# A delta-rule attention and gMLP kernel: one written-out list of steps, 16x16 blocks joined on TensorE, packed grams, loads in halves

## The chip, the cores and the metric

The kernel runs on one core of one Trainium2 chip. Its engines here are TensorE (PE, with PEld for its weight loads), VectorE (DVE), ScalarE (ACT), GpSimd (POOL) and SyncE (SP, which only issues DMAs). The metric is device microseconds (us) of one execution, lower is better; the median of the runs is compared.

## What is computed

Attention with the delta rule runs over 768 tokens for 4 x 8 heads with 48 dimensions, then a gated MLP with a matmul over the tokens:

```python
k_n = k / (norm(k) + 1e-06)
for t in range(S):                                    # S = 768, state is 48x48 per head
    y[:, :, t] = einsum('bhd,bhde->bhe', q[:, :, t], state)
    v_old = einsum('bhde,bhd->bhe', state, k_n[:, :, t])
    state = state + bt * einsum('bhd,bhe->bhde', k_n[:, :, t], v[:, :, t] - v_old)
x = y.transpose(0, 2, 1, 3).reshape(B, S, H * D)      # 4 x 768 x 384
h = gelu_tanh(x @ w_in)                               # 1024 columns
u, v = h[..., :512], h[..., 512:]
v_n = (v - mean(v)) / sqrt(var(v) + 1e-06) * g_ln
v_s = einsum('ts,bsd->btd', w_sg, v_n) + b_sg[None, :, None]
return x + (u * v_s) @ w_out
```

## The kernel before

**Tiling.** The 768 tokens are cut into 12 chunks of 64 tokens, six for each of two batch halves (phases). A chunk holds 32 heads as 16 pairs `j` on 128 partitions, and its pairs come in two groups e = 0 and 1 (two batches that the state passes through one after the other). Two chunks are a segment. Inside a chunk the recurrence is solved with the inverse of a 64x64 unit triangular matrix per head, built from the gram matrix of the keys.

**The inverse.** `kgram` and `gram` make the grams on PE; ACT copies them to `gm` (L225, L272, L295); `gstore` (L240) sends their 32x32 diagonal blocks to DRAM (`gd`, 64 KB each, four per chunk); `zload` (L306) brings them back as `zl`, one 32x32 block per partition. `lanes(g)` then inverts all blocks of a group of segments at once on DVE: norms by Newton steps (L176 to L184), `scale` (L352), an elimination over 30 pivots with `row` (L357), `column` (L362), `outer` (L368) and `add` (L375), `last` (L396). Groups 0 and 1 are one segment each (chunks 0 and 1, chunks 2 and 3), groups 2 and 3 two segments each. `zstore` (L421) writes the blocks to `zd`, and `zfetch` reads them per chunk: two DMAs for `zk` (L430), four for the tile `z` (L435). `turned` transposes `zk` on DVE (L444). `corner_a` and `corner_b` compute the off-diagonal 32x32 quarter on PE, 32 matmuls each, with an ACT copy `j` (L461) between and four ACT copies of `z` behind (L478).

**The chain of a chunk.** For e = 0 and 1: `old` (PE, then DVE adds into `v`, L510), `own` (PE, ACT copies `u`, L532), `state` and `read` (PE, ACT copies `s`, L545, and `x`, L560). The state `s` of one step feeds the next `old`. All these matmuls stand on one line of a helper, L81, as do the grams and corners.

**The MLP.** `Ffn(c)` of a finished chunk: `turn` (transposes L664, `xh` on ACT, `xl` on DVE L668), `values` (18 matmuls, L678, gelu on ACT, `bn_stats` on DVE), `gate` (four times nine matmuls, L642 to L644, gelu L699). The weight `w_in` comes in six pieces that DVE decodes, about nine operations each (L584 to L602, ACT cast L594). After the last chunk come the norm, the matmul over tokens (`spatial`) and the output (`project`); this tail is the same code in both kernels.

**What sets the order.** The program is written in the order in which each engine runs it. `TURNS` says which chunk's chain runs with which chunk's `Ffn`; a fixed body places every step of a turn. The DVE work of `lanes` and the decoding stand in a list `bg`, and `tick` lets them out by a budget of microseconds per step (`SHARE`, `COST`). Nearly all DMAs are issued by SP, in program order: a DMA whose data isn't there holds all behind it. The fetch of `z` for a chunk is made at the head of the turn if its segment is stored by then, and again at its end.

Of the kernel before, what the change touches and what calls it, by code (L numbers as in the profile page):

```python
# [50 lines left out]
TURNED = {0: 0, 1: 1, 3: 2, 4: 3, **{c + 2: c for c in range(4, NCH)}}  # L51
# [3 lines left out]
def delta_rule_gmlp_kernel(  # L55
# [63 lines left out]
    GM = [(main if i < 4 else low).tile([P, NP, 2, T], F32, name=f"gm{i}") for i in range(N_M)]  # L119
# [19 lines left out]
    loads = [nc.sync]

    def kload(c):
        if c < NCH:
            load(loads[0], KD[c % N_2], kqT[c])

    def qload(c):
        if c < NCH:
            load(loads[0], KQ[c % N_2], kqT[c])

    def tload(c):
        if c < NCH:  # L150
            load(loads[0], KT[c % N_2], ktok[c])

    def vload(c):
        if c < NCH:
            load(loads[0], V[c % N_2], vtok[c])

    bg, credit = [], [0.0]

    def tick(us):

        credit[0] += us
        while bg and credit[0] >= bg[0][1]:
            f, cost = bg.pop(0)
            credit[0] -= cost
            f()
        if not bg:
            credit[0] = 0.0
# [44 lines left out]

    def kgram(c):
        def phase(e):
# [16 lines left out]
    def gstore(c, queues):  # L231
# [5 lines left out]
        for half in range(2):  # L237
            for sd in range(2):
# [39 lines left out]
    def gram(c):  # L278
# [4 lines left out]
        def phase(qd):  # L283
# [10 lines left out]
            def done():  # L294
                nc.scalar.copy(out=GM[c % N_M][:, js], in_=st["ps"])  # L295
# [5 lines left out]
    def zload(s):  # L301
        if s >= NSEG:
            return
        if s % 2 == 0:
            zsrc[0] = prep.tile([P, 2, 32, 32], F32, name="zl")
        nc.sync.dma_start(  # L306
            out=zsrc[0][:, s % 2], in_=gdt.pop(s).rearrange("a b c j s t -> (a b c j) s t"))

    def lanes(g):
# [5 lines left out]
        st = {}  # L315

        n = prep.tile([P, m, 32], F32, name=f"n{m}", bufs=2)
        nb = prep.tile([P, m, 32], F32, name=f"nb{m}")
        d0 = prep.tile([P, m, 32], F32, name=f"d0{m}")
        tv = nc.vector  # L320

        def triu():
            (nc.scalar.copy if g < 1 else tv.tensor_copy)(out=d0, in_=dg)
            for a in range(m):
# [3 lines left out]
                )  # L328

# [35 lines left out]

        def outer(i, r0, r1, at):
            w = 31 - i
            tv.tensor_tensor(  # L368
                out=st["tmp"][:, at:at + m * (r1 - r0) * w].rearrange("p (m r t) -> p m r t", m=m, t=w),
                in0=z[:, :, r0:r1, i:i + 1].broadcast_to([P, m, r1 - r0, w]),  # L370
                in1=z[:, :, i:i + 1, i + 1:32].broadcast_to([P, m, r1 - r0, w]), op=ALU.mult)

        def add(i, r0, r1, at):
            w = 31 - i
            tv.tensor_tensor(  # L375
                out=z[:, :, r0:r1, i + 1:32], in0=z[:, :, r0:r1, i + 1:32],
                in1=st["tmp"][:, at:at + m * (r1 - r0) * w].rearrange("p (m r t) -> p m r t", m=m, t=w),
                op=ALU.add)

        us = lambda n: (0.13 if m == 1 else 0.17) + n / 960  # L380
        ops = [(f, us(32 * m)) for f in first] + [(scale, m * us(1024))]
        for i in range(1, 31):
            w = 31 - i
            if i <= N_ROWS[m]:
                ops += [(lambda a=a, r=r, i=i: row(a, r, i), us(w)) for r in range(i) for a in range(m)]
            elif w <= N_COLS[m]:
                ops += [(lambda a=a, t=t, i=i: column(a, t, i), us(i)) for t in range(i + 1, 32) for a in range(m)]
            else:
                parts = [(0, i // 2, 0), (i // 2, i, 256)] if m == 1 else [(0, i, 0)]
                ops += [(lambda i=i, p=p, f=f: f(i, *p), us(m * (p[1] - p[0]) * w)) for f in (outer, add) for p in parts]  # L390
            if g == 0 and i == 28:
                ops.append((lambda: tv.tensor_copy(out=kick[:, 0:8], in_=z[:, 0, 0, 20:28]), us(8)))
# [752 lines left out]
```

## Time and profile before

| what | value |
|---|---|
| median of 3 runs | 538.41 us (537.6 to 540.06) |
| the profiled execution: its own time is its span | 538.2 us |
| PE busy | 441.4 us (82%) |
| DVE busy | 346.6 us (64%) |
| ACT busy | 171.8 us (32%) |
| POOL busy | 74.9 us (14%) |
| chain that ended last | PE 61%, DVE 17%, DMA 7%, issue 7%, ACT 4%, SP's queue 4% |

The page of the profile gives each engine's busy time and the chain of work that ended last, followed back from the last instruction. The shares are averages; the stages differ, and the stretches below are cut at events of the program: the first operation of the first inversion (18.7 us), its store (47.2), the second `v` add of chunk 3 (155.9), the first of chunk 4 (200.4) and the start of the last part's steady run (378.0).

### The profile page before, as it was taken

The page shows a single profiled execution, that of the slowest core. Times are in us where ns is not written, and L with a number is a line of the kernel's source. Part 1 is how long each engine was busy: PE and PEld are TensorE (multiplying, and loading weights), DVE is VectorE, ACT ScalarE, POOL GpSimd, SP SyncE. Part 2 cuts the span into 40 slices and gives each one's busy share as a digit, 9 for nine tenths or more (in the row PEclk, how much of TensorE's full clock was granted, in tenths as well). Part 3 has the DMA queues.
Part 4 walks back from the last instruction along what each step waited for, and adds up shares of the span by engine and source line. Part 5 has one row for each costly group of instructions (what it writes and reads, how often), then busy time and mean ns, then how long its engine had stood idle before and what let it go on. Part 6 is the DMA issues. An engine that isn't in the chain of part 4 may idle for free.

```text
span 538.2 us, 17698 instructions
## 1 busy us (share of the span) xinstructions
PE 441.4 (82%) x7691; PEld 395.2 (73%) x7691; DVE 346.6 (64%) x858; ACT 171.8 (32%) x383; POOL 74.9 (14%) x87
## 2 busy tenths in 40 slices
PE   4316785570889949898989896999998999999997
PEld 2316475470778748687777775878898999999997
DVE  3999999648997229689913359643599636623332
ACT  3222333230423522333533533444534213211110
POOL 2100002102201004010010110000024223222130
PEclk9555756555599969899999998899999999999999
DMA  7987858965538796645955868265857753344204
GB/s 181 278 199 195 179 156 211 248 174 126 156 95 237 218 206 165 195 117 165 314 146 155 277 154 250 65 202 163 246 161 187 214 166 104 103 147 147 74 16 132
DMA packets 111965, 93.18 MB, mean 173 GB/s; under 512 B 74768, under 2 KB 88016, under 8 KB 111888
## 3 DMA queue, kind: packets, MB, share of 16 engines
q1 hardware_dynamic: 101504, 68.23, 45.3%
q0 software_dynamic: 6032, 22.28, 15.0%
q10 hardware_dynamic: 4352, 1.54, 1.2%
q8 instruction: 60, 0.98, 0.8%
q14 instruction: 17, 0.14, 0.1%
HBM read 63.69 MB, written 28.34 MB: 171 GB/s over the span
## 4 chain that ended last, share of the span: by engine, by line
PE 61%; DVE 17%; DMA 7%; issue 7%; ACT 4%; SPq 4%; ACTq 1%; DVEq 0%
PE ps L81 19%; PE ps L642 12%; PE ps L644 11%; PE ps L643 11%; PE ps L678 8%; DVE ztmp L368 3%; DVE zl L375 3%; DMA kd<-kqT 2%; DMA vraw<-vD 2%; PE ps L664 1%; DMA gd<-gm 1%; DMA zl<-gd 1%; SPq L752 1%; ACT gm L295 1%; DVE zl L357 1%
## 5 line engine op out<-in xcount | busy, mean ns | idle before, releaser
L81 PEld LDWEIGHTS ps<-s,kq 48*64 48x64 f32 x1408 | 55.8, 159 | 21.3 <-issue 14.8
L81 PE MATMUL ps<-s,kq 48*64 48x48 f32 x1408 | 63.1, 245 | 9.7 <-issue 8.3
L785 POOL TENSOR_TENSOR ga<-ga,uT 128x384 f32<-128x384 f32 x32 | 36.3, 1140 | 165.8 <-DVE ga L782 120.9
L81 PE MATMUL ps<-kd 48*64 48x128 f32 (+1 forms) x768 | 40.2, 337 | 19.4 <-DMA kd<-kqT 17.4
L81 PE MATMUL ps<-v,z 64*64 64x48 f32 x768 | 33.7, 244 | 23.2 <-DVE v L510 13.8
L81 PEld LDWEIGHTS ps<-kd 48*64 48x64 f32 x768 | 33.8, 177 | 22.9 <-DMA kd<-kqT 15.3
L81 PEld LDWEIGHTS ps<-v,z 64*64 64x64 f32 x768 | 30.4, 159 | 24.5 <-DVE v L510 14.4
L368 DVE TENSOR_TENSOR ztmp<-zl 128x120 f32<-128x120 f32 (+25 forms) x132 | 45.9, 372 | 2.2
L375 DVE TENSOR_TENSOR zl<-zl,ztmp 128x120 f32<-128x120 f32 (+25 forms) x132 | 45.7, 370 | 1.6
L642 PE MATMUL ps<-xh,winh 128*128 128x256 f32 x144 | 45.7, 317 | 0.9 <-DVE xl L668 0.9
L643 PE MATMUL ps<-xl,winh 128*128 128x256 f32 x144 | 42.1, 293 | 0.4 <-DVE xl L668 0.3
L644 PE MATMUL ps<-xh,winl 128*128 128x256 f32 x144 | 41.8, 290 | 0.0
L647 ACT CAST gh<-ga 128x384 fp32r<-128x384 f32 x32 | 16.3, 511 | 77.3 <-POOL ga L785 63.3
L81 PE MATMUL ps<-u,gm 64*64 64x48 f32 x768 | 34.1, 245 | 2.6 <-ACT u L532 1.9
L648 DVE TENSOR_TENSOR gl<-ga,gh 128x384 fp32r<-128x384 f32 x32 | 18.1, 565 | 26.8 <-ACT gh L647 26.7
L532 ACT COPY u<-ps 128x384 f32<-128x384 f32 x24 | 11.5, 479 | 70.6 <-PE ps L81 70.6
L644 PE MATMUL ps<-wouth,gl 128*128 128x384 f32 x96 | 32.3, 340 | 1.5 <-DVE gl L648 1.5
L81 PEld LDWEIGHTS ps<-u,gm 64*64 64x64 f32 x768 | 30.2, 159 | 4.4 <-ACT u L532 2.4
L642 PE MATMUL ps<-wsgh,vnh 128*128 128x384 f32 x96 | 32.7, 340 | 0.7 <-ACT vnh L755 0.6
L81 PE MATMUL ps<-u,kt 64*48 64x48 f32 x704 | 27.3, 234 | 6.4 <-issue 4.6
L643 PE MATMUL ps<-wsgl,winh 128*128 128x384 f32 x96 | 32.5, 339 | 0.0
L642 PE MATMUL ps<-wsgh,winh 128*128 128x384 f32 x96 | 32.5, 339 | 0.0
(127 smaller groups left out, 1097.2 us busy)
## 6 DMA issues: line engine op xcount, KB each, us to landing
kq<-kqT POOLq DMA_DIRECT2D x10, 896.0 KB, 6.8
uD<-ut SPq DMA_DIRECT2D x12, 512.0 KB, 5.2
vD<-vg SPq DMA_DIRECT2D x24, 256.0 KB, 4.0
vraw<-vD SPq DMA_DIRECT2D x48, 128.0 KB, 3.1
uT<-uD SPq DMA_DIRECT2D x8, 768.0 KB, 5.4
kd<-kqT SPq DMA_DIRECT2D x6, 896.0 KB, 8.3
xD<-x SPq DMA_DIRECT2D x12, 384.0 KB, 6.9
x<-xD SPq DMA_DIRECT2D x48, 96.0 KB, 2.8
```

The costliest lines, as they stand in the source:

```text
L81: return nc.tensor.matmul(out=out, lhsT=lhsT, rhs=rhs, start=start, stop=stop, skip_group_check=True)
L295: nc.scalar.copy(out=GM[c % N_M][:, js], in_=st["ps"])
L368: tv.tensor_tensor(out=st["tmp"][:, at:at + m * (r1 - r0) * w].rearrange("p (m r t) -> p m r t", m=m, t=w), in0=z[:, :, r0:r1, i:i + 1].br ...
L375: tv.tensor_tensor(out=z[:, :, r0:r1, i + 1:32], in0=z[:, :, r0:r1, i + 1:32], in1=st["tmp"][:, at:at + m * (r1 - r0) * w].rearrange("p (m ...
L532: ins = mark(nc.scalar.copy(out=u[:, js[e]], in_=ub[e]))
L642: nc.tensor.matmul(out=ps, lhsT=sh, rhs=mh, start=(first and i == 0), stop=False)
L643: nc.tensor.matmul(out=ps, lhsT=sh, rhs=ml, start=False, stop=False)
L644: nc.tensor.matmul(out=ps, lhsT=sl, rhs=mh, start=False, stop=(last and i == n - 1))
L647: nc.scalar.copy(out=hi, in_=src)
L648: nc.vector.tensor_tensor(out=lo, in0=src, in1=hi.bitcast(F32), op=ALU.subtract)
L678: nc.tensor.matmul(out=self.ps, lhsT=(self.xl if k == 2 else self.xh)[:, cc, bi], rhs=(winl if k == 1 else winh)[:, cc, DH:], start=(i == ...
L785: nc.gpsimd.tensor_tensor(out=gv, in0=gv, in1=uT[:, :, d], op=ALU.mult)
```

## The change

- **One list.** `TURNS`, `tick`, `SHARE` and `COST` are gone. `PROGRAM` is a list of 490 words such as `old:0:4` or `l:22` (the next 22 operations of `lanes` in `bg`) or `d:1` (the next part of the decoding), done one by one. Every load and store names its queue, S (SP), A (ACT) or P (POOL). DMAs issued by SP go from 353 to 303, by ACT from 10 to 54, by POOL from 37 to 68.
- **16x16 blocks.** For groups 0 and 1 `lanes` inverts two 16x16 blocks per 32x32 block: 28 multiplies and adds in a row. `join` makes the 32x32 inverses from them for chunks 0 to 3, on PE, with two masked copies and an add on DVE and four ACT copies per chunk; both halves of `zk` are fetched and transposed there.
- **Packed grams.** `gm` is split in keys (packed in 32-token halves) and queries. Two neighbouring heads then stand side by side, and a corner takes 16 matmuls instead of 32; `corner_a` ends in a masked copy on DVE (L504) instead of the ACT copy, `corner_b` in two ACT copies instead of four. Each quarter of a gram is copied by two ACT copies (L236, L331) instead of one.
- **Loads.** `kd` and `kq` are loaded in halves of 448 KB; each load waits for the last marked copy (of `u` or `s`) before it in the list. `z` is fetched once per chunk.
- **Moved.** No decoding stands ahead of the first inversion; the first `values` and `gate` steps stand inside the chain of chunk 2, not of chunk 3.

```diff
-TURNS = ((0, None), (1, None), (2, None), (3, 0), (None, 1), (None, 2),
-         *((c, c - 1) for c in range(4, NCH)), (None, NCH - 1))
+PROGRAM = """
+keys:1:S keys:0:A consts beta:A kq:1:0:P kq:1:1:S kgram:0 kgram:1 kd:3:1:S gstore:0:S:A gstore:1:P kd:3:0:P kq:0:0:S
+kick:12 zload:0:A kd:2:1:A l:1 kd:2:0:A qgram:1 lanes:0 gram:3 kd:5:0:P gram:2 warm:9 kq:0:1:P w:0:A kt:0:P
...
+l:6 turn:2 v:4:S kt:4:S vprep:4 l:2 kd:11:0:A own:1:3 l:1 ustore:0 gate:1:0 values:1:17 gate:1:1 kd:10:0:S
+gstore:8:S:P gstore:9:S:P kd:11:1:P kq:5:1:P state:1:3 gate:1:2 gate:1:3 v:5:P ustore:1 gate:2:0 gram:11 gate:2:1
+blocks:4:S:P l:5 xstore:2 heads:4:S:A:P gate:2:2 gate:2:3 turn:3 values:2:16 mask:7 kt:5:S corner_a:4 gram:10 turned:4
+gstore:10:S mask:6 old:0:4 zload:4:S vprep:5 mask:8 gate:3:0 values:2:1 heads:5:S:P corner_b:4 norms:3 gstore:11:S
...
+        if marked:
+            tc.add_manual_dep(
+                ins.ins, marked[0].ins.name,
...
+        nblk, w0 = (2 * m, 16) if small else (m, 32)
...
         def outer(i, r0, r1, at):
-            w = 31 - i
+            w = w0 - 1 - i
             tv.tensor_tensor(
-                out=st["tmp"][:, at:at + m * (r1 - r0) * w].rearrange("p (m r t) -> p m r t", m=m, t=w),
-                in0=z[:, :, r0:r1, i:i + 1].broadcast_to([P, m, r1 - r0, w]),
-                in1=z[:, :, i:i + 1, i + 1:32].broadcast_to([P, m, r1 - r0, w]), op=ALU.mult)
+                out=products(i, r0, r1, at),
+                in0=zb[:, :, r0:r1, i:i + 1].broadcast_to([P, nblk, r1 - r0, w]),
+                in1=zb[:, :, i:i + 1, i + 1:w0].broadcast_to([P, nblk, r1 - r0, w]), op=ALU.mult)
...
+        def one(half):
+            ps = bank().rearrange("p (i x t) -> p i x t", x=2, t=32)
+            for i in range(8):
+                for sd in range(2):
...
+                    mm(ps[TOK[sd], i], g[b, half, x].rearrange("p x t -> p (x t)"),
+                       z[b, x, 32 * half:32 * half + 32])
+            y[half] = main.tile([P, 8, 2, 32], F32, name="j1", bufs=2)
+            head_pairs(y[half], ps, same_upper)
...
         for i in range(8):
-            for odd in range(2):
-                for sd in range(2):
-                    a = slice(64 * sd + 32 * odd, 64 * sd + 32 * odd + 32)
-                    b = slice(64 * sd + 32, 64 * sd + 64)
-                    j = 2 * i + odd
-                    mm(ps[a, i], g[b, j, 0, 0:32], z[b, j, 32:64])
-        nc.scalar.copy(out=j1, in_=ps)
+            for sd in range(2):
+                b = slice(64 * sd + 32, 64 * sd + 64)
+                x = slice(2 * i, 2 * i + 2)
+                mm(ps[TOK[sd], i], g[b, 0, x].rearrange("p x t -> p (x t)"), z[b, x, 32:64])
+        head_pairs(j1, ps, same)
```

On DVE, at the first elimination, where `zl` holds the blocks, `ztmp` the products and `nb` the factors per token, the kernel before has, behind its `scale`:

```order
L352 TENSOR_TENSOR zl<-zl,nb_253 128x1024
L357 SCALAR_TENSOR_TENSOR zl<-zl 128x30
L357 SCALAR_TENSOR_TENSOR zl<-zl 128x29 x2
L357 SCALAR_TENSOR_TENSOR zl<-zl 128x28 x3
L357 SCALAR_TENSOR_TENSOR zl<-zl 128x27 x4
```

and the changed kernel, at the same place:

```order
L396 TENSOR_TENSOR zl<-zl,nb_285 128x2x16x16
L420 TENSOR_TENSOR ztmp<-zl 128x28
L427 TENSOR_TENSOR zl<-zl,ztmp 128x2x14
L420 TENSOR_TENSOR ztmp<-zl 128x52
L427 TENSOR_TENSOR zl<-zl,ztmp 128x2x2x13
```

The 36 single rows and columns and 76 halves of products and adds have become 28 operations, each on both small blocks of all partitions.

On SP's queue, around the fetch of chunk 4's blocks (`z_104` and `zk`), the kernel before has:

```order
L240 DMA gd<-gm_98 32x16x32 x4
L685 DMA vD_75<-vg 128x512
L430 DMA zk<-zd 64x8x32 x2
L435 DMA z_104<-zd 32x16x32 x4
L704 DMA uD_77<-ut 128x2x512
L685 DMA vD_75<-vg 128x512
L240 DMA gd<-gm_99 32x16x32 x4
L685 DMA vD_75<-vg 128x512
L430 DMA zk<-zd 64x8x32 x2
L435 DMA z_104<-zd 32x16x32 x4
```

and the changed kernel, where the other half of these fetches stands on POOL's and ACT's queues:

```order
L267 DMA gd<-gm_97 32x16x32 x2
L807 DMA uD_77<-ut 128x2x512
L470 DMA zd<-zl 128x1024 x2
L476 DMA z_104<-zd 32x16x32 x2
L812 DMA xD_73<-x 128x2x384
L476 DMA zk<-zd 64x8x32
L788 DMA vD_75<-vg 128x512
```

The second fetch of the same blocks, behind the store of the last gram `gm_99`, is gone, and the fetch stands right behind the store `zd`.

On ACT, between the two copies `u` of chunk 0's chain, the kernel before has:

```order
L532 COPY u<-ps 128x384
L545 COPY s_112<-ps 112x384
L560 COPY x<-ps 128x384
L295 COPY gm_102<-ps 128x512
L532 COPY u<-ps 128x384
```

and the changed kernel:

```order
L638 COPY u<-ps 128x384
L267 DMA gd<-gm_100 32x16x32 x2
L721 DMA ut<-w_in 128x2x512
L651 COPY s_112<-ps 112x384
L666 COPY x<-ps 128x384
L172 DMA kd_95<-kqT 112x2x512
L638 COPY u<-ps 128x384
```

DMA issues now stand on ACT between the copies on which the chain of the chunks hangs.

## Rows read from the trace of the kernel before

**Rows 1.** The page: busy us of each engine, share of the span, instructions.

```profile
PE 441.4 (82%) x7691; PEld 395.2 (73%) x7691; DVE 346.6 (64%) x858; ACT 171.8 (32%) x383; POOL 74.9 (14%) x87
```

**Rows 2.** Stretches: length, busy us by engine, granted clock, DMA share, GB/s.

```profile
0.00:18.70 18.70, 6.11 (x137) 3.12 (x137) 9.91 (x20) 4.91 (x8) 3.58 (x13) 0.82 0.72 193
18.70:47.20 28.50, 13.05 (x317) 12.40 (x321) 27.43 (x133) 6.91 (x16) 1.23 (x1) 0.56 0.89 242
47.20:155.90 108.70, 70.28 (x1948) 59.94 (x1941) 91.12 (x248) 34.80 (x78) 14.65 (x18) 0.58 0.72 175
155.90:200.40 44.50, 36.27 (x602) 31.34 (x601) 21.87 (x45) 17.51 (x43) 1.44 (x2) 0.92 0.74 198
200.40:378.00 177.60, 161.25 (x3830) 135.40 (x3831) 111.96 (x260) 70.89 (x177) 17.70 (x22) 0.96 0.63 182
378.00:538.20 160.20, 154.46 (x869) 153.01 (x867) 84.32 (x155) 36.73 (x63) 36.34 (x32) 1.00 0.46 141
```

**Rows 3.** Timeline of DVE: first and last operation of the first elimination (start, us).

```profile
24.66 1.48 DVE L357 SCALAR_TENSOR_TENSOR zl<-zl 128x30 f32<-128x30 f32 x8
...
45.79 0.09 DVE L400 MEMSET zl<- 128x32 f32 x1
```

**Rows 4.** Groups of DVE by line and shape: count, busy us, mean ns of one.

```profile
L396 DVE TENSOR_TENSOR zl<-zl,nb 128x1024 f32<-128x1024 f32 x6 | 7.1, 1213 | 0.0
L444 DVE STREAM_TRANSPOSE ztk<-zk 128x256 f32<-128x256 f32 x12 | 5.3, 438 | 3.5 <-DMA zk<-zd 3.5
L598 DVE TENSOR_TENSOR ut<-ut,vg 128x512 f32<-128x512 f32 x6 | 4.2, 693 | 0.2
L368 DVE TENSOR_TENSOR ztmp<-zl 128x112 f32<-128x112 f32 x4 | 1.1, 266 | 0.0
```

**Rows 5.** What DVE waited for, 47.2 to 155.9: us in total, times, longest.

```profile
DVE d L323 <- DMA zl<-gd: 8.6, 1, 8.6
DVE vg L584 <- DMA ut<-w_in: 3.8, 1, 3.8
```

**Rows 6.** Timeline of DVE: chunk 3's second `v` add, chunk 4's first.

```profile
155.87 0.55 DVE L510 TENSOR_TENSOR v<-v,ps 128x384 f32<-128x384 f32 x1
...
200.44 0.56 DVE L510 TENSOR_TENSOR v<-v,ps 128x384 f32<-128x384 f32 x1 [5.36 <-PE ps L81]
```

**Rows 7.** Timeline ahead of chunk 4: last gram store, fetch, first corner (idle before, releaser).

```profile
188.41 2.01 SPq L240 DMA_DIRECT2D gd<-gm  x4
...
191.00 1.29 SPq L430 DMA_DIRECT2D zk<-zd  x2
...
195.67 1.29 PE L81 MATMUL ps<-z,gm 32*32 32x32 f32 x64 [6.81 <-DMA z<-zd]
```

**Rows 8.** The chain of waits, 150 to 180: start, us, what.

```profile
156.89 1.08 PE ps L81 x64
...
166.36 0.12 PE ps L644
...
167.91 1.84 PE ps L678 x8
```

**Rows 9.** Timeline of PE at full clock: a whole gram, a corner.

```profile
173.43 1.98 PE L81 MATMUL ps<-kd 48*64 48x128 f32 x64
...
279.38 0.75 PE L81 MATMUL ps<-z,gm 32*32 32x32 f32 x64
```

**Rows 10.** What PE waited for, 200.4 to 378.

```profile
PE ps L81 <- issue: 11.4, 10, 2.6
```

**Rows 11.** Timeline of ACT and PE around ACT's issues of chunk 0's fetch.

```profile
50.54 1.39 ACTq L435 DMA_DIRECT2D z<-zd  x2
51.97 1.56 ACT L295 COPY gm<-ps 128x512 f32<-128x512 f32 x3 [7.86 <-issue]
...
52.61 1.75 PE L81 MATMUL ps<-kd 48*64 48x128 f32 x26 [2.03 <-ACT gm L295]
```

**Rows 12.** A stretch inside the first elimination, columns as in Rows 2.

```profile
20.00:30.00 10.00, 6.11 (x137) 5.78 (x141) 9.35 (x48) 4.76 (x12) 0.00 (x0) 0.67 1.09 292
```

More of the change, by code (lines that the diff above doesn't have):

```diff
@@ new lines @@
+old:0:1 gstore:6:S:A:P d:2 kd:8:1:A own:0:1 turned:2 join:1:2 d:2 gram:7 join:2:2 state:0:1 kq:2:0:S old:1:1 d:1
+own:1:1 mask:4 join:3:2 turn:0 mask:2 v:2:S corner_a:2 state:1:1 d:1 blocks:3:S:P turn:1 join:0:3 gstore:7:S:A:P
+corner_b:2 d:2 join:1:3 heads:3:S kd:9:0:A kd:8:0:P zload:2:P turned:3 zload:3:S bglanes:2 gram:8 v:3:S d:1 l:1
+kq:2:1:A kd:9:1:S l:2 vprep:2 xstore:1 old:0:2 gram:9 kt:2:A join:2:3 kq:3:0:S own:0:2 l:3 kq:3:1:A l:1 kd:10:1:S l:22
+l:3 vprep:3 values:0:6 join:3:3 state:0:2 old:1:2 gate:0:0 own:1:2 l:12 kt:3:P corner_a:3 state:1:2 old:0:3 l:10
@@ L135, in load, with behind @@
         flat = tile.rearrange("p j t -> p (j t)") if len(tile.shape) == 3 else tile.rearrange("p i j t -> p (i j t)")
-        q.dma_start(
+        ins = q.dma_start(
             out=flat.rearrange("p (n x) -> p n x", x=src.shape[-1]), in_=src.rearrange("n p x -> p n x"))
[L139 to L167, printed above, removed]
+        if marked:
+            tc.add_manual_dep(
+                ins.ins, marked[0].ins.name,
+                mybir.DependencyInfo(mybir.DependencyClass.Sync, mybir.DependencyReason.DATA),
+                reason="loads are spread over the turn")
+    queues = {"S": nc.sync, "A": nc.scalar, "P": nc.gpsimd}
+    bg = []
+    def behind(n):
+        for _ in range(min(n, len(bg))):
+            bg.pop(0)[0]()
     def until(ready):
@@ L373, in add @@
         def add(i, r0, r1, at):
[L374 to L378, printed above, removed]
+            z_ = zb[:, :, r0:r1, i + 1:w0]
+            tv.tensor_tensor(out=z_, in0=z_, in1=products(i, r0, r1, at), op=ALU.add)
         us = lambda n: (0.13 if m == 1 else 0.17) + n / 960
-        ops = [(f, us(32 * m)) for f in first] + [(scale, m * us(1024))]
@@ L388, in lanes @@
             else:
[L389 to L392, printed above, removed]
+                parts = [(0, i // 2, 0), (i // 2, i, 256)] if m == 1 and not small else [(0, i, 0)]
+                ops += [(lambda i=i, p=p, f=f: f(i, *p), us(nblk * (p[1] - p[0]) * w) + (0.08 if small else 0.0))
+                        for f in (outer, add) for p in parts]
@@ L818, in delta_rule_gmlp_kernel, with keys, make_constants, first_keys @@
+    ffns, chains, joins, units, held, units_w = {}, {}, {}, [], {}, []
+    def keys(c, q):
+        load(q, KD[c % N_2][:, 0], kqT[c, 0:2])
+    def make_constants():
+        make_identity(nc, ident)
+        for z in Z:
+            for r in range(2):
+                nc.gpsimd.memset(z[64 * r + 32:64 * r + 64, :, 0:32], 0.0)
+    def first_keys(c):
         k0, k1 = kgram(c)
         deal([k0], [k1])
[L820 to L822 removed]
@@ new lines, in link, with chain_of, joined, transposed @@
+    def link(name, c, new=None):
+        chain_of(c, new)[name]()
+    def chain_of(c, new):
+        if c not in chains:
+            chains[c] = chain(c, new)
+        return chains[c]
+    def joined(k, c):
+        if c not in joins:
+            joins[c] = join(c)
+        joins[c][k]()
+    def transposed(c):
+        ffns[c] = Ffn(c)
+        ffns[c].turn()
+    def gated(c, d):
+        decoded(len(win) - 9)
+        ffns[c].gate(d)
+    def valued(c, n):
+        decoded(len(win))
+        ffns[c].values(n)
@@ new lines, in key_norms, with decoded, all_lanes, lanes_in @@
+    def key_norms(s):
+        until(lambda: s in ns)
+        norms(s)
+    def decoded(n):
+        for _ in range(n):
+            win.pop(0)[0]()
+    def all_lanes(g):
+        for op, _ in lanes(g):
+            op()
+    def lanes_in(s, q):
+        if s % 2 == 0 and s:
+            lanes_done(s - 1)
+        zload(s, q)
+    def blocks_in(c, qs):
+        lanes_done(c // 2)
+        zblocks(c, spread(qs))
+    def heads_in(c, qs):
+        lanes_done(c // 2)
+        zheads(c, spread(qs))
```

569 lines of the change are left out of this document (266 added, 303 removed).

## The prediction, made before the changed kernel ran

> **What bounds the kernel now.** I read the page's busy line first, then the stretches, then inside each stretch what its late engine waits for. PE is busy for 441.4 us of 538.2 [rows 1], so the whole gain to be had by removing idle time is under 97 us, and the stretches say where those lie [rows 2]. In the last one PE works 154.5 of 160.2 us at clock 1.00: nothing to gain. From 200.4 to 378.0 it works 161.3 of 177.6 at 0.96. From 155.9 to 200.4 it works 36.3 of 44.5, and 6.8 of what is missing is one wait, ahead of chunk 4's first corner, for the blocks `z` [rows 7]. Before 155.9 PE is no bound: 89.4 of 155.9 busy, at clock 0.56 to 0.58 for most of it, while DVE is 27.4 of 28.5 and 91.1 of 108.7 busy. So DVE's queue sets when chunk 3 ends, chunk 4's blocks then set when PE can go on, and from there PE is the bound. I cut the run at DVE's `v` adds [rows 6] and write it as A (start to chunk 4's first add, 200.4) + B (to 378.0, 177.6) + C (160.2) = 538.2, the profiled execution's own time; the median of the runs, 538.41, is 0.2 above it.
>
> **A, DVE up to chunk 3's second add (155.9).** *Small blocks.* An elimination took from 24.66 to 45.79 plus 0.09, 21.1 us [rows 3]. The new one is 28 operations, 2240 elements per partition in all. From the 112 and 512 element rows [rows 4], 0.266 and 0.693 us, an operation costs about 0.149 + n/960, so 28 x 0.149 + 2.33 = 6.5. Each waits for the one ahead, where the old halves overlapped; no row prices that apart, so I bound it by 0 and 0.1 us each and take 0.04: 7.6 (6.5 to 9.3). `scale` and `last` fall from 1.21 (the row of 1024 elements, [rows 4]) to 0.69, 1.0 for the pair. That is 14.5 per group; two groups, **-29.0**. *Added.* A joined chunk costs DVE two masked products of 512 elements (0.69 each), a second transpose (0.44) and a small add (under the 0.27 of 112 elements plus what PSUM adds; 0.3): 2.1, four chunks **+8.5**. The masked corner copy moves from ACT to DVE, 0.69 x 4 = **+2.8** here (x 12 in all). One mask is taken a chunk earlier, 1024 elements, **+1.2**. *Moved.* The decoding that stood ahead of the first elimination filled a wait: DVE was 9.9 us busy in 0 to 18.7 [rows 2], and about 10 of that now follows the elimination, **+10**. Is the elimination then earlier? It waits for the grams' trip through DRAM, which remains; I leave its start at 18.7 (17 to 21). The sum is -6.5 of DVE work. Idle time in this part was 12.4 us in two waits [rows 5], one for the blocks of lanes, one for a piece of `w_in`; the same two loads remain in another order, so I keep it (6 to 20). So 155.9 - 6.5 = **149.4** (143 to 157). The large eliminations of groups 2 and 3 are not touched.
>
> *Is PE able to follow?* It gets the joins: per chunk 64 + 64 + 32 passes of 32 columns or fewer, at the corner's 0.75 per 64 [rows 9] up to 1.9 us, at half clock 3.8, four times 15. It gets some 14 `values` and 3 `gate` steps that stood behind 155.9: at 0.23 (1.84 for 8) and 1.1 (nine at 0.12) [rows 8], doubled for the clock, 6.4 + 6.6. 89.4 + 15 + 13 = 117 us of work in 149.4: it fits, but no longer loosely. ACT gets sixteen-row copies and twice the gram copies, at under 0.15 us more per pair: 35 us of 108.7 was its load [rows 2].
>
> **A, from there to chunk 4 (44.5 before).** At full clock I count what stands in the new list between `old:1:3` and `old:0:4`: 33 `values` x 0.23 = 7.6; 8 gates x 1.2 = 9.6; two whole grams x 1.98 [rows 9] = 4.0; two turns, own, state, old and the corner, by the 1.08 of 64 passes [rows 8], about 6. That is 27 to 28, against some 34 by the same count before, plus the waits. The 6.8 for `z` [rows 7] goes if the blocks are there: the second elimination pair ends as far behind chunk 3's second add as before, 16 us of DVE work, so at about 166; a store and a fetch then need some 8 (the fetch took 191.0 to 195.7 [rows 7], the store by its position about 3): 174. The corner comes about 25 us behind 149.4, at 174. So it is met, just; what is late next is the corner itself. Fetching once, ahead of the last gram store (188.4 [rows 7]), is what makes that possible. 149.4 + 28 = **177** (171 to 188), against 200.4.
>
> **B.** Seven corners: 32 passes of 64 columns instead of 64 of 32. Passes took 11.7 ns at 32 columns [rows 9], 16.9 at 48 [rows 8] and 31 at 128 [rows 9], so I take 20 at 64: 0.64 against 0.75, 0.11 twice per chunk, -1.6; the ACT copies behind them get shorter too, in all **-2**. PE's idle time is 16.3, of it 11.4 in ten waits at issue [rows 10], and 4% of clock on 161 us is 6 more. A new interleaving moves these; nothing in a row says by how much, so between 0 and two thirds (15) I take **-6**, since no wait is long (2.6 at most) and DVE with 112 of 177.6 is no bound. 177.6 - 8 = **169.6** (163 to 178).
>
> At the corners a rule speaks for more. The rows say that passes follow their columns. The Trainium skill, "TensorEngine Tiling (Array Packing)", section "Instruction Overhead", states that each matmul has about 60 cycles of overhead and that one column costs as much as 60. By it halving the calls would halve the corners, 0.75 in place of 0.22 saved per chunk, and the sum would be 3.7 lower; the trace disagrees between 32 and 48 columns.
>
> **C.** The last part is the same code with PE at 154.5 of 160.2: **160.2** (159 to 162).
>
> **Sum: 177 + 169.6 + 160.2 = 507 us.** By the ends of the three parts, which need not fall together, 493 to 528.
>
> **Rivals.**
> *PE's gaps close.* If the new list also fills the waits that I kept (chunk 4 at 171, the lower end, and B at 163): 171 + 163 + 160.2 = **494** (485 to 497). For it: PE worked 70 of 108.7 us at half clock in the middle, so there is room. Against: it needs DVE's waits gone, too.
> *PE and DVE wait in turn.* The 28 us of joins and early MLP work may not fit under DVE's queue, since chain steps need one engine, then the other, and PE had 38.4 idle in 47.2 to 155.9 [rows 2] for that reason. If half of it adds up, chunk 4 is at 177 + 14.5 = 191.5 and the time is **522** (515 to 533). For it: DVE's and PE's loads are 131 and 117 of 149.
> *The DMA engines are the bound early.* Their share was 0.72 to 0.89 up to 200 [rows 2] and 1.09 in 20 to 30 [rows 12]; the change cuts eliminations, not bytes. Then lanes start no earlier, halves or not, A stays at 200.4 and only B's 8 is gained: **530** (530 to 539); without B's gain no change. For it: the three long waits named above are all for a DMA. Against: 0.72 from 47.2 to 155.9 leaves a quarter of the engines' time. The Trainium skill, "DMA: Bandwidth & Descriptors", section "Issuing engines are not separate DMA queues", says that DMAs of ScalarE, SyncE and GpSimd run on the same 16 engines and that more issuers only save issue time; it speaks for this rival, and no row here, with nearly all issues on SP, shows it.
> *Slower: ACT as an issuer.* When ACT issued the fetch of chunk 0's blocks, its gram copies stood 7.86 us behind, and PE 2.03 behind them [rows 11]. The new list puts 22 issues on ACT between the first join and chunk 4's corner, between copies of `u` and `s`, each waiting for a landing or for the DMA eight issues earlier. If each costs the chain that 2.03, 45 us come on top: **552**. It decides from 1.55 us per issue on ((541.1 - 507) / 22). Against: most of these waits are for landings long past when ACT arrives.
>
> **How the numbers follow.** Forecast 0.45 (497 to 515), gaps closed 0.15, waiting in turn 0.20, DMA bound 0.08, ACT as issuer 0.12. A change of under 0.5%, 2.7 us (535.7 to 541.1), can't be told from none by runs that spread over 2.5. Faster: 0.45 + 0.15 + 0.20 and a quarter of 0.08: 0.82. Same: the rest of the DMA case, 0.06. Slower: 0.12. The range goes from 488, which leaves out the lower part of the closed gaps, to 536, which leaves out the ACT case and the DMA case's upper part: 0.8 lie inside.
>
> **What would show it.** Right: the first elimination starts near 18.7 and takes 8 us; chunk 3's second add near 149, chunk 4's first near 177, with no long wait of PE for `z` ahead of it; the last part 160 long. Wrong: idle time of ACT ahead of `u` or `s` behind its own issues (the slower case); a first elimination well behind 21, or waits of DVE for `zl` above 12 us (DMA); PE and DVE both under 80% busy from 50 to 150 with waits on each other (in turn); `z` of chunk 4 landing behind 180, then the second half of the gain in A is lost.

## The result, and the profile after

The changed kernel takes 513.85 us (median of 4, 512.55 to 516.31) against 538.0 beside it: ratio 0.9545, 95% interval 0.9501 to 0.9589, 24.5 us faster. The forecast was 507 (488 to 536). Medians are of all executions, ratios only of those in the chip's faster state. The profiled execution took 510.8 us, against 538.2, so 27.4 have to be found there.

The page of the changed kernel, busy time and the chain that ended last by engine:

```profile
PE 452.8 (89%) x7563; PEld 414.5 (81%) x7563; DVE 332.4 (65%) x728; ACT 171.8 (34%) x403; POOL 92.7 (18%) x120
...
PE 74%; DMA 13%; DVE 7%; ACT 3%; issue 2%; SPq 1%; POOL 0%; ACTq 0%; POOLq 0%; DVEq 0%
```

PE is busy for 11 us more than in [rows 1], and the run is shorter: PE's idle time fell from 97 to 58 us. The two `v` adds at which the prediction cut the run, in DVE's timeline of the changed kernel:

```profile
154.82 0.55 DVE L616 TENSOR_TENSOR v<-v,ps 128x384 f32<-128x384 f32 x1 [0.48 <-PE ps L115]
...
181.63 0.54 DVE L616 TENSOR_TENSOR v<-v,ps 128x384 f32<-128x384 f32 x1
```

Chunk 3's second add stands where it stood [rows 6], 1.05 us earlier; chunk 4's first is 18.8 earlier. The rest is shown by cutting both runs at these adds and at the first matmul over the tokens. First the kernel before, then the changed one (columns as in [rows 2]; a granted clock of 1.00 is 2.4 GHz, 0.50 is 1.2 GHz):

```profile
0.00:155.87 155.87, 89.42 (x2394) 75.44 (x2395) 128.43 (x398) 46.59 (x102) 19.46 (x31) 0.61 0.75 190
155.87:200.44 44.57, 36.34 (x602) 31.41 (x602) 21.90 (x45) 17.54 (x43) 1.44 (x2) 0.92 0.74 198
200.44:378.88 178.44, 162.09 (x3834) 136.08 (x3834) 112.60 (x262) 71.74 (x179) 17.70 (x22) 0.96 0.63 182
378.88:538.20 159.32, 153.58 (x865) 152.29 (x863) 83.67 (x154) 35.88 (x60) 36.34 (x32) 1.00 0.46 141
```

```profile
0.00:154.82 154.82, 112.75 (x2844) 98.67 (x2845) 112.46 (x267) 55.22 (x148) 37.69 (x61) 0.77 0.71 190
154.82:181.63 26.81, 26.81 (x443) 24.34 (x444) 20.56 (x41) 12.23 (x34) 5.33 (x8) 1.00 0.89 268
181.63:354.30 172.67, 160.31 (x3415) 139.08 (x3414) 118.90 (x275) 70.56 (x164) 14.00 (x19) 0.97 0.69 198
354.30:510.80 156.50, 152.92 (x866) 152.41 (x864) 80.46 (x149) 33.77 (x59) 35.71 (x32) 1.00 0.48 144
```

In the first stretch nothing is gained in time, but PE is busy for 23 us more, and at a granted clock of 0.77 against 0.61. Most of that is not later work but the joins, as PE's groups in this stretch of the changed kernel show:

```profile
L115 PE MATMUL ps<-z,gm 32*64 32x64 f32 x384 | 18.1, 266 | 11.8 <-DMA z<-zd 11.8
L115 PE MATMUL ps<-j,ztk 64*32 64x32 f32 x256 | 6.6, 230 | 0.3 <-DVE ztk L501 0.3
L115 PE MATMUL ps<-ztk,j 64*64 64x16 f32 x128 | 6.0, 236 | 0.0
```

The last two rows are joins alone, the first is too but for four corners (6.2 us): 24.5 us in all. Steps of `values` and `gate` that stood later take 18.1 us here against 8.8, so 9.3 us of later work is done; the rest of PE's work took some 10 us less, at the higher clock. The second stretch then is PE work alone, busy without a gap at full clock: it is shorter by the 8.2 us of idle time that it had and by 9.5 us of work. The third gives 5.8 us, the last 2.8.

What PE waited for, over the whole changed kernel and, in the second fence, over the kernel before (us, times, longest; a wait at "issue" is idle time for which the profile names no other engine or DMA):

```profile
PE ps L115 <- DMA kd<-kqT: 19.3, 3, 9.8
PE ps L115 <- DMA z<-zd: 11.8, 3, 10.6
PE ps L115 <- DVE j L504: 4.9, 1, 4.9
PE ps L115 <- issue: 4.5, 3, 3.5
```

```profile
PE ps L81 <- issue: 21.6, 16, 3.4
PE ps L81 <- DMA kd<-kqT: 17.4, 5, 13.3
PE ps L81 <- DVE v L510: 13.8, 4, 12.1
```

Gone are the wait for `v` adds (13.8, now 3.0), most of the waits at issue, and the 6.8 for chunk 4's `z` [rows 7]. New are 10.6 for chunk 0's blocks (PE reaches the first join before they are there) and 4.9 for the masked corner copy `j`, which stands on DVE behind the start of the last inversion.

### The profile page after: what moved, and what is told of

It reads as the page before. It is cut to its first block, busy times and chain, and to the rows that moved or that the text cites. A ratio compares the mean times of both kernels' runs of the same rounds, so it can differ in the third digit from the quotient of the medians.

```text
span 510.8 us, 17402 instructions
## 1 busy us (share of the span) xinstructions
PE 452.8 (89%) x7563; PEld 414.5 (81%) x7563; DVE 332.4 (65%) x728; ACT 171.8 (34%) x403; POOL 92.7 (18%) x120
## 4 chain that ended last, share of the span: by engine, by line
PE 74%; DMA 13%; DVE 7%; ACT 3%; issue 2%; SPq 1%; POOL 0%; ACTq 0%; POOLq 0%; DVEq 0%
PE ps L115 23%; PE ps L745 14%; PE ps L747 13%; PE ps L746 13%; PE ps L781 9%; DMA gd<-gm 3%; DMA zl<-gd 3%; DMA kd<-kqT 3%; DMA kq<-kqT 2%; PE ps L767 1%; DVE ztmp L420 1%; DVE zl L427 1%; SPq L267 1%; DMA z<-zd 1%; DMA v<-vtok 1%
## 5 line engine op out<-in xcount | busy, mean ns | idle before, releaser
L115 PE MATMUL ps<-s,kq 48*64 48x48 f32 x1408 | 54.4, 228 | 4.6 <-ACT s L651 3.5
L115 PEld LDWEIGHTS ps<-s,kq 48*64 48x64 f32 x1408 | 48.2, 142 | 11.7 <-issue 4.9
L115 PE MATMUL ps<-kd 48*64 48x128 f32 (+1 forms) x768 | 33.4, 350 | 22.9 <-DMA kd<-kqT 19.3
L115 PEld LDWEIGHTS ps<-kd 48*64 48x64 f32 x768 | 30.3, 191 | 24.2 <-issue 16.4
L115 PE MATMUL ps<-z,gm 32*64 32x64 f32 x640 | 27.5, 248 | 12.2 <-DMA z<-zd 11.8
L420 DVE TENSOR_TENSOR ztmp<-zl 128x28 f32<-128x28 f32 (+20 forms) x84 | 36.0, 428 | 2.7
L427 DVE TENSOR_TENSOR zl<-zl,ztmp 128x28 f32<-128x28 f32 (+20 forms) x84 | 35.9, 427 | 2.4
L115 PEld LDWEIGHTS ps<-z,gm 32*64 32x64 f32 x640 | 24.6, 158 | 14.9 <-issue 12.4
L747 PE MATMUL ps<-wsgh,winl 128*128 128x384 f32 x96 | 32.5, 339 | 0.0
L745 PE MATMUL ps<-wouth,gh 128*128 128x384 f32 x96 | 32.3, 339 | 0.0
```

Of the source, the lines that this page charges most:

```text
L115: return nc.tensor.matmul(out=out, lhsT=lhsT, rhs=rhs, start=start, stop=stop, skip_group_check=True)
L420: tv.tensor_tensor(out=products(i, r0, r1, at), in0=zb[:, :, r0:r1, i:i + 1].broadcast_to([P, nblk, r1 - r0, w]), in1=zb[:, :, i:i + 1, i ...
L427: tv.tensor_tensor(out=z_, in0=z_, in1=products(i, r0, r1, at), op=ALU.add)
L745: nc.tensor.matmul(out=ps, lhsT=sh, rhs=mh, start=(first and i == 0), stop=False)
L747: nc.tensor.matmul(out=ps, lhsT=sl, rhs=mh, start=False, stop=(last and i == n - 1))
```

## The experiments

Ratios are to the kernel before, with their 95% intervals; the changed kernel's is 0.9545. Differences between two of them carry both intervals. The edits are shown in extracts: `...` stands for lines left out, and of a line of the list only the words around the change are shown.

**The small blocks undone.**

```diff
-SMALL = (0, 1)
+SMALL = ()
...
-heads:1:P kd:5:1:S l:1 gram:5
+heads:1:P kd:5:1:S l:3 gram:5
...
```

> The changed kernel, but groups 0 and 1 are inverted as whole 32x32 blocks again and the joins are gone; the list of steps keeps its order (the counts of inversion steps that are let out of the list in chunk 0 and 1 are stretched by 2.6, as there are more steps). Theory: DVE's queue was what the small blocks shortened, by 29.0 us less 8.5 for the joins; about 15 to 20 us come back, 529 to 534 us, ratio to before 0.983 to 0.992, and the first inversion takes 21 us instead of 7.7. Rival: joins, their PE work and their waits take as long as the large elimination did, and the gain is the order alone: 510 to 518 us, ratio 0.948 to 0.963.

534.27 us, ratio 0.9895 (0.9806 to 0.9984): 3.5% slower than the changed kernel, 18.8 us (13 to 24). The theory holds. The first inversion's end and two adds in its trace (chunk 3's second, chunk 4's first):

```profile
48.83 0.09 DVE L449 MEMSET zl<- 128x32 f32 x1
...
173.17 0.55 DVE L616 TENSOR_TENSOR v<-v,ps 128x384 f32<-128x384 f32 x1 [4.02 <-PE ps L115]
201.02 0.55 DVE L616 TENSOR_TENSOR v<-v,ps 128x384 f32<-128x384 f32 x1
```

The inversion ends 13.5 us later than in the changed kernel (35.3), chunk 3's add 18.4 later, chunk 4's 19.4. So what DVE saves on the two small groups, 29.0 less 8.5, reaches the end nearly whole; and this list without the small blocks is worth about 1%, no more than the single fetch below. A list written for the longer inversions was not tried.

**The joins left out.**

```diff
-        if c not in JOINED:
-            return []
+        return [lambda: None] * 4
```

> The changed kernel without the four join steps of chunks 0 to 3: their matmuls, masked copies, adds and ACT copies are left out, so the inverses of these chunks are not computed fully; all else stays. It prices the joins. Theory: the joins stand on the chain of chunks 0 to 3, at 15 us of PE at half clock and 6 us of DVE; the time falls by 10 to 15 us, to 499 to 504, ratio 0.928 to 0.937. Rival: they lie beside other waits: it falls by under 4, ratio above 0.947.

509.88 us, ratio 0.9431 (0.9359 to 0.9503): 6.1 us less than the changed kernel, with 4.5 of uncertainty. That lies between the two theories and touches both: part of the joins is covered, and less than half of the 24.5 us that they take of PE alone is on the path.

**One fetch in the kernel before.**

```diff
-            zfetch(n, nc.sync)
+            if n not in zks:
+                zfetch(n, nc.sync)
```

> The kernel before, with the second fetch of chunk 4's blocks left out (the same blocks were fetched twice). Theory: PE's wait of 6.8 us ahead of chunk 4's first corner goes, the corner comes at about 190 instead of 195.7, and the time falls by 5 to 6: 532 to 533 us, ratio 0.988 to 0.991. Rival: PE finds another wait there (the ready work is used up), under 1 us, ratio above 0.997.

534.31 us, ratio 0.9901 (0.9863 to 0.9939), 5.3 us, as the theory said. The corner that waited 6.81 for `z` until 195.67 [rows 7] now reads, in PE's timeline, with chunk 4's add on DVE behind it:

```profile
188.18 0.75 PE L81 MATMUL ps<-z,gm 32*32 32x32 f32 x64
...
193.59 0.55 DVE L510 TENSOR_TENSOR v<-v,ps 128x384 f32<-128x384 f32 x1 [2.67 <-PE ps L81]
```

The wait for `z` is gone, and the add is 6.9 us earlier.

**The corners undone.**

```diff
         for i in range(8):
-            for sd in range(2):
...
-                mm(ps[TOK[sd], i], g[b, 0, x].rearrange("p x t -> p (x t)"), z[b, x, 32:64])
-        head_pairs(j1, ps, same)
+            for odd in range(2):
+                for sd in range(2):
...
+                    mm(ps[a, i], g[b, 0, j], z[b, j, 32:64])
+        nc.scalar.copy(out=j1, in_=ps)
...
```

> The changed kernel with the corners as before: 32 matmuls of 32 columns instead of 16 of 64 for each, an ACT copy behind corner_a instead of the masked one on DVE, four ACT copies behind corner_b instead of two; packed grams and the rest stay. Theory: passes follow their columns, so the new form saves 0.11 us twice per chunk and some ACT time, some 2 to 3 us over 12 chunks: 515.5 to 517, ratio 0.957 to 0.961. Rival: the masked copy on DVE (8.3 us in all) costs more than ACT's did, as DVE is the fuller engine ahead of chunk 4: 510 to 513, ratio 0.947 to 0.953.

527.57 us, ratio 0.9794 (0.9744 to 0.9844): 13.4 us slower than the changed kernel (10 to 17), far from either expectation. A corner in PE's timeline at full clock, of the changed kernel and then with the old corners:

```profile
239.47 1.15 PE L115 MATMUL ps<-z,gm 32*64 32x64 f32 x32
```

```profile
225.44 0.75 PE L115 MATMUL ps<-z,gm 32*32 32x32 f32 x64
```

Taken by itself the new corner is slower: 1.15 us for half the passes (a pass is one matmul record; a matmul here makes two). So what it saves is not pass time. PE's waits at issue and PE's page line with the old corners, and the first and third stretch, cut at the same events as above:

```profile
PE ps L115 <- issue: 19.9, 16, 4.9
...
PE 465.6 (88%) x8331; PEld 425.0 (81%) x8331; DVE 324.0 (61%) x716; ACT 179.8 (34%) x439; POOL 92.7 (18%) x120
```

```profile
0.00:164.30 164.30, 119.92 (x3100) 106.06 (x3101) 110.80 (x263) 58.05 (x160) 37.68 (x61) 0.70 0.68 179
...
192.40:370.13 177.73, 166.47 (x3899) 143.07 (x3900) 115.34 (x268) 75.11 (x188) 14.02 (x19) 0.92 0.68 193
```

With the old corners 15.4 us of waits at issue come back (19.9 against 4.5), but as other waits get shorter, PE's idle time rises by 3.4 us only (58.0 to 61.4). What makes the run longer is PE's busy time: 465.6 us against 452.8, for less pass time, at a granted clock of 0.70 against 0.77 in the first stretch and 0.92 against 0.97 in the third. Behind chunk 4's first add the clock falls to 1.2 GHz four times, three of them within 2 us behind a wait at issue, and once in the changed kernel; that these waits bring the clock down is likely, but not shown by itself.

Where most of these waits come from, the traces do show. The instructions of PE are loaded by DMA while it runs, on queue q8; the page's line of the changed kernel, then with the old corners:

```profile
q8 instruction: 59, 0.97, 0.8%
```

```profile
q8 instruction: 65, 1.06, 0.9%
```

That is one load for 256 of PE's instructions (a matmul and a weight load per pass: 2 x 7563 and 2 x 8331; 60 loads for 2 x 7691 before). Of the 16 waits at issue with the old corners 14, and of the 17 in the kernel before (16 in the row above, one on another line) 16, end between 2.0 and 3.1 us behind the start of such a load; of all moments between 20 and 350 us 16% to 18% lie so. So most of these are waits of PE for its own instructions, and with half the corners' calls they are rare. The other parts of the edit, the masked copy and the number of ACT copies, were not tested apart.

**The new waits moved.** In the changed kernel PE waits 9.8 us for chunk 9's keys near 114 to 123.5. The gram that needs them was moved:

```diff
-old:0:2 gram:9 kt:2:A join:2:3
+old:0:2 kt:2:A join:2:3
...
-old:1:2 gate:0:0 own:1:2
+old:1:2 gate:0:0 gram:9 own:1:2
```

> The changed kernel with one word of the list moved: the gram of chunk 9 stands behind the first gate of chunk 0's MLP instead of behind chunk 2's first old step. There PE waited 9.8 us for the keys of chunk 9. Theory: the wait is on the path, what stands behind it comes up to 9.8 us earlier, and the time falls by 5 to 9: 505 to 509 us, ratio 0.938 to 0.947. Rival: DVE, 40.1 of 44.8 us busy in that stretch, is the bound there and the wait is idle time that costs nothing: 512 to 516, ratio 0.951 to 0.959.

515.43 us, 0.955 (0.9495 to 0.9604): no change. PE's longest wait in 110 to 155 now is

```profile
PE ps L115 <- DMA kq<-kqT: 8.3, 1, 8.3
```

another load of the same burst of issues at 114 us. So that load was moved up, too, and then the third inversion's first operations were put behind the `v` add:

```diff
-kq:2:0:S old:1:1
+kq:2:0:S kq:2:1:S old:1:1
```

> The changed kernel with two moves in the list: chunk 9's gram behind the first gate of chunk 0's MLP, and the second half of chunk 2's queries loaded 25 words earlier, by SP right behind the first half. With the gram alone moved, PE's wait of 9.8 us for keys became one of 8.3 us for these queries, which were issued at 114.8. Theory: the two waits were one DMA burst at 114 us, PE can now go on, and chunk 4's first add comes 5 to 8 us earlier: 506 to 509 us, ratio 0.940 to 0.947. Rival: DVE's queue (40 of 45 us busy) holds that stretch whatever PE does: 512 to 516, ratio 0.951 to 0.959.

518.25 us, 0.9622 (0.9561 to 0.9683).

```diff
-d:1 l:1 kq:2:1:A kd:9:1:S l:2 vprep:2 xstore:1 old:0:2
+d:1 kd:9:1:S vprep:2 xstore:1 old:0:2 l:3
```

> The kernel of the run before (chunk 9's gram later, chunk 2's queries earlier) with one thing more: the first three operations of the third inversion stand behind chunk 2's first v add on DVE instead of ahead of it. There DVE, which runs in order, waited for the blocks of that inversion (zl, until 117.7 in the changed kernel, 121.4 in the run before), and the ready v add stood behind it. Theory: this wait, not DVE's work, set chunk 2's first add; the add comes at 116 to 118 instead of 121.3 and 125.0, and 3 to 7 us reach chunk 4: 507 to 511 us, ratio 0.942 to 0.950. Rival: the third inversion then starts later and chunk 4's blocks are late by as much: 513 to 518, ratio 0.954 to 0.963.

517.01 us, 0.9562 (0.9502 to 0.9621). Both theories fell: neither is faster than the changed kernel. The first of the two (e10) shows what took the place of the waits, on DVE and then on PE:

```profile
121.35 0.22 DVE L364 COPY d<-zl 128x64 f32<-128x64 f32 x1 [5.04 <-DMA zl<-gd]
...
125.03 0.55 DVE L616 TENSOR_TENSOR v<-v,ps 128x384 f32<-128x384 f32 x1
...
125.69 0.34 PE L115 MATMUL ps<-v,z 64*64 64x48 f32 x2 [6.75 <-issue]
```

PE stands for 6.75 us again, now for chunk 2's first add. The profile books it at issue, but these matmuls read the `v` that the add writes. DVE did the add at 125.0 instead of 121.3, since it waited 5.0 us for the blocks of the third inversion first (1.6 in the changed kernel). Besides, PE's clock is lower; 110 to 155 in the changed kernel and in e10:

```profile
110.00:155.00 45.00, 32.79 (x887) 29.21 (x882) 40.27 (x80) 17.42 (x45) 5.85 (x7) 0.85 0.59 176
```

```profile
110.00:155.00 45.00, 34.03 (x773) 30.50 (x773) 37.92 (x75) 15.06 (x37) 5.85 (x7) 0.70 0.50 149
```

PE is busy for longer (34.0 against 32.8) with fewer instructions. In the last run (e11), made against that wait, chunk 2's first add did come at 115.4, and the time is no lower for it; what took the gain there stays open.

**Is it the clock?** The waits were filled with matmuls that nobody reads:

```diff
-mask:3 qgram:0 blocks:0:S:P
+mask:3 qgram:0 warm:44 blocks:0:S:P
...
-old:0:2 gram:9
+old:0:2 warm:42 gram:9
```

> The changed kernel with idle matmuls added in PE's two longest waits: 44 in the wait for chunk 0's blocks (32.9 to 43.5 us) and 42 in the wait for chunk 9's keys (113.7 to 123.5); they write a bank that nobody reads. Behind both waits PE ran at half clock in the changed kernel (43.5 to about 57, 123.5 to 129.7), though it ran at full clock ahead of them. Theory: the clock fell in the waits, and this, not the waits alone, is what the early part and the runs with the moved gram paid (granted clock 0.62 to 0.70 in 110 to 155 there, 0.85 in the changed kernel): behind the filled waits the clock stays at 1.00, the joins take half as long, and chunk 4's first add comes 3 to 7 us earlier: 507 to 511 us, ratio 0.942 to 0.950. Rival: what follows the waits is held by DVE and by DMAs anyway, or the clock falls all the same: 513 to 517, ratio 0.954 to 0.962.

521.74 us, 0.9692 (0.965 to 0.9735): slower by 7.9. PE's timeline around the first filled wait:

```profile
33.41 9.67 PE L132 MATMUL ps<-busy 128*128 128x512 bf16 x43
...
45.73 1.90 PE L115 MATMUL ps<-z,gm 32*64 32x64 f32 x62 [0.52 <-DMA z<-zd]
49.55 1.97 PE L115 MATMUL ps<-j,ztk 64*32 64x32 f32 x64 [1.92 <-DVE ztk L501]
```

The first join ran in 1.90 us instead of 3.31, as wished, but at 49.55 the clock had halved all the same (64 passes of this join take 1.11 at full clock), right behind the stretch at full clock. The fall was moved, not avoided. In the second wait the clock had fallen before the idle matmuls began, and the gram behind them came at 131.1 instead of 123.55; they may have held it up themselves. So whether the lower clock ate a part of what the moved waits gave is not shown by this run.

**The first inversion's start.** It began at 22.35 instead of 18.72. Three runs went after it, by the queues, by the warming and by using DVE's idle time there:

```diff
-kgram:1 kd:3:1:S gstore:0:S:A gstore:1:P
+kgram:1 gstore:0:S:A gstore:1:S:A
...
+kick:12 zload:0:A kq:1:0:P kq:1:1:S kd:3:1:S kd:3:0:P kq:0:0:S
```

> The changed kernel with its first loads and stores as before: the gram stores of chunk 1 go out on SP and ACT instead of POOL, and the loads of chunk 0's and 1's queries and chunk 3's keys stand behind the first load of the blocks. The first inversion started at 22.35 us instead of 18.72. Theory: POOL's four issues (12.13 to 14.71) and the early loads made it late; it starts near 19, and as nothing later takes the gain, the time falls by 2 to 4: 510 to 512, ratio 0.947 to 0.952. Rival: the loads moved behind are then late themselves and the gain is gone by chunk 1: 513 to 516, ratio 0.953 to 0.960.

518.13 us, 0.9636 (0.958 to 0.9692): 4.9 us slower than the changed kernel (1 to 9). The inversion started at 23.4. The edit did not do what it was made for: POOL and SP still issued those loads at 10.5 to 15.8, ahead of the load of the blocks on ACT's queue at 18.4. And the blocks' trip had become longer. Stores of the grams and load of the blocks up to 22 us, with the us from issue to landing last, in the kernel before and in the changed one:

```profile
gd<-gm SPq DMA_DIRECT2D x4, 64.0 KB, 2.7
zl<-gd SPq DMA_DIRECT2D x1, 512.0 KB, 3.3
```

```profile
gd<-gm POOLq DMA_DIRECT2D x4, 64.0 KB, 3.8
zl<-gd ACTq DMA_DIRECT2D x1, 512.0 KB, 4.1
```

Here they took 4.6 and 4.7. That the early loads beside them make it longer is the obvious rival, and no run kept these loads away.

```diff
-kq:1:1:S kgram:0 kgram:1
+kq:1:1:S warm:9 kgram:0 kgram:1
...
-gram:2 warm:9
+gram:2
```

> The changed kernel with the nine warming matmuls moved back ahead of the first gram, where the kernel before has them. Theory: the first grams ran at half clock (128 passes in 3.69 us, 2.10 before) since nothing ran ahead of them, and this is 1.6 us of the 3.6 by which the first inversion starts later; with the move they take 2.1 and it starts near 20.8; the time falls by 1 to 2 us: 512 to 513, ratio 0.950 to 0.954. Rival: the start follows the DMAs alone (stores and loads of the blocks share the engines with the early loads): it stays at 22 or more and the time at 514, ratio 0.954 to 0.957.

516.47 us, 0.9573 (0.9516 to 0.963): no difference. The grams took 3.03 us instead of 3.69, the start stayed at 22.2.

```diff
-consts beta:A kq:1:0:P
+consts beta:A w:0:S kq:1:0:P
...
-qgram:1 lanes:0
+qgram:1 d:3 lanes:0
```

> The changed kernel with the first piece of w_in loaded at once by SP and decoded by DVE ahead of the first inversion, as the kernel before did: DVE stood idle for 19.2 us there, and the piece took 6 us behind the inversion. Theory: DVE's queue is shorter by about 6 us from 36 us on, the masks of chunks 0 and 3 and the joins come earlier, 1 to 4 us less: 510 to 513, ratio 0.947 to 0.953. Rival: the 512 KB more in the first 20 us delay the blocks' trip by 1 us or more and it comes out slower: 514 to 517, ratio 0.955 to 0.962.

516.08 us, 0.9586 (0.9551 to 0.9621): no difference; chunk 2's first add came at 121.6 (121.3 in the changed kernel), so 6 us of DVE work taken out of the queue early were lost to waits by then.

**ACT's DMA issues.**

```diff
-heads:2:S:A
+heads:2:S:S
```

and so for 15 other words of that part; ACT issues 33 DMAs instead of 54, so it was 21 that moved, not 22.

> The changed kernel with all DMAs that ACT issued between the first join and chunk 4's corner (22) given to SP. Rival of the prediction: each issue on ACT held up a copy on the chain; even at a third of the 2.03 us priced ahead, 15 us would be gained. Theory: these issues cost ACT little (its waits for a DMA sum to about 11 us between 37 and 155, most beside other waits), and SP's queue, which then waits for the landings in order, gives them back: within 4 us, 510 to 518, ratio 0.948 to 0.962.

517.19 us, 0.9632 (0.958 to 0.9684): 4.7 us slower than the changed kernel (1 to 8), a little beyond the range expected. The slower rival of the prediction is refuted: the issues on ACT are worth a little.

## Why the prediction was right, and where it was off

The direction, the cut and most steps held. By its own terms:

- *Elimination.* 7.6 us forecast, 7.8 measured. In DVE's timeline of the changed kernel, first operation, first product, end:

```profile
22.35 0.18 DVE L198 TENSOR_SCALAR rsq_y<-d 128x32 int32<-128x32 int32 x1 [19.21 <-ACT d L364]
...
27.64 0.19 DVE L420 TENSOR_TENSOR ztmp<-zl 128x28 f32<-128x28 f32 x1
...
35.34 0.09 DVE L449 MEMSET zl<- 128x32 f32 x1
```

- *DVE's work to chunk 3's second add.* Forecast -6.5; busy time from the first inversion's start fell from 118.6 to 110.8, -7.8.
- *Start kept at 18.7.* This step failed: 22.35, outside its bounds of 17 to 21. With 3 us more of idle time (21.7 against 18.6, both with the short gaps between operations) it makes up for 6.7 of the 7.8 saved, and chunk 3's second add came at 154.8, not 149.4. The prediction put no price on the moved warming and the early loads. The first grams, in the kernel before and in the changed one:

```profile
6.28 2.10 PE L81 MATMUL ps<-kd 48*64 48x64 f32 x128 [0.99 <-DMA kd<-kqT]
```

```profile
7.02 3.69 PE L115 MATMUL ps<-kd 48*64 48x64 f32 x128 [7.02 <-DMA kd<-kqT]
```

  0.7 us later and 1.6 longer. But neither warming nor queues alone brought the start back: the load of the blocks, issued at 14.7 in the kernel before, is issued at 17.9 here, at 17.9 with the warming and at 18.4 with the other queues. The grams end 2.3 us later, and the longer trip of the blocks above takes the rest; what makes the trip longer stays open.
- *From there to chunk 4.* 28 forecast, 26.8 measured, without a wait for `z`. Right, and most of what A gained was gained here: PE had done 9.3 us of this work ahead of chunk 3's add, part of it at a clock that rose some 18 us sooner. The joins took 24.5 us of PE there, not the 15 of the prediction, which read all their passes as 32 columns or fewer (the rows above have 64 in 256 of them); they fitted in all the same. In steps of 5 us, the changed kernel, then the kernel before:

```profile
125.00:130.00 5.00, 5.00 (x157) 4.60 (x152) 4.69 (x11) 3.84 (x12) 0.00 (x0) 0.52 0.26 85
130.00:135.00 5.00, 4.50 (x150) 3.79 (x144) 4.72 (x11) 1.61 (x5) 0.00 (x0) 1.00 0.56 166
```

```profile
145.00:150.00 5.00, 4.13 (x66) 3.60 (x61) 4.79 (x9) 2.25 (x3) 0.00 (x0) 0.63 1.07 297
150.00:155.00 5.00, 4.74 (x128) 3.93 (x127) 4.76 (x8) 1.72 (x4) 0.00 (x0) 1.00 0.61 138
```

- *A in all.* 177 forecast, 181.6 measured.
- *B and C.* 169.6 + 160.2 = 329.8 forecast, 329.2 measured, but by other terms: B was 3.1 longer than forecast and C 3.7 shorter, and that these cancel is luck. The corners' -2 was the mis-sized one: by pass time they cost more (1.15 against 0.75 [rows 9], where I had worked out 0.64 from columns), and undoing them costs 13.4. The 20 ns for a pass of 64 columns was near for tiles of 48x64, 1.16 us for 64 passes in the changed kernel, but on 32x64 tiles the pass takes 36: columns alone don't set the price.

```profile
31.76 1.16 PE L115 MATMUL ps<-kq 48*64 48x64 f32 x64
```

  The waits at issue of [rows 10], 11.4 us, which I took to be half gone for no named reason, are 0.4, and 4.9 come back with the old corners. Against that stands the new wait of 4.9 for the masked copy. C gave 2.8, of which 2.1 are two waits of PE (1.5 for `gl`, 0.6 for `vnh`) that are no longer there. By the rule weighed in the prediction (the Trainium skill, "TensorEngine Tiling (Array Packing)", section "Instruction Overhead") a corner would take half of 0.75, an estimated 0.38 us; the trace disagrees with 1.15.
- *Rivals.* ACT as issuer and the DMA bound fell (the latter by the 18.8 us of the small blocks, though its sign, a first elimination well behind 21, did show). "In turn" isn't seen either: PE and DVE are 82% and 84% busy from 50 to 150, PE waited 3.0 us for `v` adds in the whole run, and the joins left out gave 6.1, not 14.5; PE's long waits ahead of chunk 3's end, 9.8 and 10.6, are for DMAs.

Three figures of the prediction are off without changing its result: the old elimination takes 21.2 us by its rows, not 21.1; "in turn" adds up to 521, not 522; and the 131 us given as DVE's load up to chunk 3's second add is the time from 18.7 to 149.4, while its work by the prediction's own terms is 112 (118.6 - 6.5) and was 110.8, which makes "in turn" less likely than it looks there.

The effects don't add: undoing the small blocks costs 18.8, undoing the corners 13.4, and the single fetch gave 5.3 in the kernel before, 37.5 together against 24.5.

## What to carry to other kernels

Where one engine's queue sets a stage, shortening that queue is paid nearly in full: 20.5 us less of DVE work gave 18.4 at the end of its stage and 18.8 at the end of the run. Against the kernel before, the date of that event had hardly moved, since a late start, new work and later work filled the time; so undo the one part and compare, and count the other engine's work done, not only dates. Price a restructured matmul by its count of instructions and by the clock as well as by its own duration: the corner became half as long again, and undoing it still cost 13 us. A long wait in a trace is no gain by itself; four runs that removed or filled the two longest waits of PE won nothing, and in one of them the trace shows the next wait in the place of the last.

## What the runs showed of the hardware

Four matmuls on 32x32 tiles with 32 columns take less PE time than two on 32x64 tiles with 64: 64 passes in 0.75 us against 32 in 1.15, both at full clock. PE's instructions come by DMA in loads of 256, and PE can run dry of them: of its waits for which the profile names no other engine, 21.6 us in 16 on the one line before and 19.9 us in 16 with the old corners in the new list, nearly all end 2.0 to 3.1 us behind the start of such a load; with half the corners' calls 4.5 us in 3 are left. And in the run with the filled waits a granted clock of 2.4 GHz, held through the first wait by idle matmuls, fell to 1.2 GHz at 48.3, some 5 us behind their end at 43.1; PE was busy for 2.2 us of that time.
